# Opening attention of two batches: three copies per head pair and the joining of two heads' rows as SBUF-to-SBUF transfers

## The chip, the core and the metric

The kernel runs on one core of one Trainium2 chip. The metric is the device time of the launch in microseconds. Three runs of the kernel before gave 1260.57, 1261.91 and 1268.36 us; the median is 1261.91 us.

## The reference

Attention with normalized q and k feeds two feed-forward layers. The inputs are 4 batches of 12 heads, 448 positions and 64 columns a head. The change touches the attention of the first two batches alone.

```python
def _attn_ref(q, k, v, g_q, g_k):
    def rmsnorm(x, g):
        rms = np.sqrt(np.mean(x * x, axis=-1, keepdims=True) + 1e-06)
        return x / rms * g
    q_n, k_n = (rmsnorm(q, g_q), rmsnorm(k, g_k))
    scale = 1.0 / np.sqrt(q.shape[-1])
    scores = scale * np.matmul(q_n, k_n.transpose(0, 1, 3, 2))
    scores = scores - np.max(scores, axis=-1, keepdims=True)
    attn = np.exp(scores)
    attn = attn / (np.sum(attn, axis=-1, keepdims=True) + 1e-09)
    return np.matmul(attn, v).astype(np.float32)

def reference(...):
    attn_out = _attn_ref(...)                       # (4, 12, 448, 64)
    x = attn_out.transpose(0, 2, 1, 3).reshape(1792, 768)
    g = x @ w_gate;  x = (g * sigmoid(g) * (x @ w_val)) @ w_out
    h = x @ w_in;    return (h * np.cos(h)) @ w_out2
```

## The kernel before, in words

The attention is done for pairs of heads, called groups here: 6 groups a batch, 24 in all. Groups 0 to 11 (the first two batches) are done in an opening stage of their own, in which the feed-forward layers begin only near the end; the later twelve are woven into the feed-forward layers. The change is in the opening stage.

The order of the program in that stage is by a step number `n`. Every group has 7 score tiles (`NS` = 7) and so takes 7 steps; `c_step(n)` (L785) emits what belongs to a step, and each operation of group g stands at a fixed offset from step 7g. The offsets of the preparation are the third dictionary of `OFF` (L85), less 12 (`CSH`); the offsets behind the products are `CEND` (L804), counted from step 7g + 8 (`CXX`). SP's queue of DMAs and POOL run exactly in that order, each waiting at its head; PE, DVE and ACT run in an order that a scheduler makes out of it when the kernel is built.

For one group the stage does this:

- `p_load` (L317) loads q and k in float32 into `rqk`; `p_sq`, `p_pow`, `p_mul` normalize; `p_khi`, `p_klo`, `p_qhi`, `p_qlo` split into a float16 high and low part in `h16`.
- `c_T` (L656) has the DMA transpose `h16` into `T`: 7 tiles of q and 7 of k, each with its high part on rows 0 to 63 and its low part on rows 64 to 127.
- `c_copy` (L661), the operation `sw` of the table, makes three copies of 64 rows by 896 float16: on DVE the low part of q into rows 0 to 63 of a tile `B` (L666), and the high part of q over the low part in `T` (L667); on ACT the high part of k into rows 0 to 63 of a tile `C` (L668).
- `c_s` (L670) makes the 7 score tiles with `T` on both sides (matmul `s<-T`), and DVE takes the maximum of each row (L680). `c_row` (L682) turns the maxima into a row by small products (`s<-id,cw`, after DVE's two operations L687 and L688) that ACT writes into rows 64 to 127 of `B` (L693).
- `c_st` (L697) makes the transposed scores minus the maximum, with `T` and then with `C` and `B` (matmuls `c<-T` and `c<-cB,cC`), and ACT takes the exponential (L713). `c_av` (L715) multiplies by v, with columns of ones beside it: one PSUM bank has head 0's output on rows 0 to 63 and its sums below, the other has the sums above and head 1's output on rows 64 to 127.
- `c_x` (L725) copies both banks to two tiles `ov` (named `co` in the rows). `c_sum` (L743) sends the sums by DMA into a 64 by 7 form, `c_inv` inverts (L752, L753), `c_out` (L755) writes the inverses to DRAM (`rc<-sm`), `c_back` (L760) reads them back onto all rows (`cr<-rc`), and `c_mul` (L766) with `c_half` (L770) multiplies each half of 64 rows by them (L774) and splits the product for the feed-forward layers (L775, `c_lo`).

Beside this the stage loads weights (`raw`), converts some of them on DVE (L936 to L938, L969) and stores them (`scr_gate`, `scr_val`). `v` goes to tiles `cV` in five DMAs a group.

The two functions on which the steps rest most are these:

```python
        nc.vector.tensor_copy(Bq[:HP], T[HP:, :NS])
        nc.vector.tensor_copy(T[HP:, :NS], T[:HP, :NS])
        nc.scalar.activation(C[:HP], T[:HP, NS:], AF.Copy)
...
        for rows, src in ((slice(0, P), ov),) if g == NC - 1 else ((slice(0, HP), ov[0]), (slice(HP, P), ov[1])):
            nc.vector.tensor_tensor(xs[rows], src[rows], r[rows], op=ALU.mult)
...
    CEND = ((c_x, 0), (c_sum, 1), (c_inv, 3), (c_out, 4), (c_back, 6), (c_mul, 8), (c_lo, CXL))
```

Of the kernel before, what the change touches and what calls it, by code (L numbers as in the profile page):

```python
# [14 lines left out]
AF = mybir.ActivationFunctionType  # L15
ALU = mybir.AluOpType
AX = mybir.AxisListType
PSUM = bass.MemoryType.PSUM
A0 = {'raw0': 2, 'h160': 1, 'sq0': 1, 'pr0': 6, 'T0': 2}
COL = {'B': 3, 'C': 3, 'w': 3, 'r': 1, 'o': 4, 'V': 2}  # L20
A1 = {'p16': 2, 'PT': 1, 'sq': 1, 'pr': 3, 'sm': 10, 'R': 1, 'rv': 1, 'raw': 1, 'h16': 1, 'T': 2}
CF = ('kl xl ql qm kf', 'rp vh nm xl qm sa 2', 'ql xl 0 2 5 6', 'ql xl 0 3 4 6')
LA = 5
# [14 lines left out]
CXL = 11  # L38
# [2 lines left out]
CC2 = 29  # L41
NPH = 3
EARLY = 75
PREL = 33
HPRE = (5, 3)
LO = 3
# [6 lines left out]
for _n, _w in ((67, ("load", 8)), (70, ("load", 9)), (74, ("conv", 8)), (78, ("conv", 9))):  # L53
# [13 lines left out]
  'T': -2,  # L67
  'vhi': -4,
  'vlo': -3,
  'sw': -1},  # L70
 {'load': -23,
  'vload': -21,
  'sqk': -18,
# [7 lines left out]
  'T': -7,  # L81
  'vhi': -10,
  'vlo': -4,
  'sw': -5},
 {'load': -23,  # L85
  'vload': 6,
  'sqk': -18,
  'sqq': -18,
  'pow': -15,
  'mul': -15,  # L90
  'khi': -15,
  'klo': -11,
  'qhi': -14,
  'qlo': -9,
  'T': -6,
  'vhi': -10,
  'vlo': -4,
  'sw': -2},
 {'load': -13,
  'vload': -12,  # L100
  'sqk': -11,
# [7 lines left out]
  'T': -4,  # L109
  'vhi': -6,  # L110
  'vlo': -2,
  'sw': -2},
 {'load': -11,
  'vload': -10,
  'sqk': -9,
# [7 lines left out]
  'T': -4,  # L123
  'vhi': -4,
  'vlo': -3,
  'sw': -2},
 {'load': -16,
  'vload': -14,
  'sqk': -14,
# [7 lines left out]
  'T': -6,  # L137
  'vhi': -7,
  'vlo': -5,
  'sw': -4})  # L140
DEL = ({'phi': 4, 'plo': 4, 'pt': 5, 'sum': 8, 'r': 8, 'av0': 8, 'av1': 9, 'av2': 9, 'av3': 10, 'x': 11},
# [30 lines left out]
def kernel(ctx: ExitStack, tc, q, k, v, g_q, g_k, w_gate, w_val, w_out, w2_in, w2_out, out):  # L172
    nc = tc.nc
    in_order = set()
    sync = InOrder(tc, nc.sync, "SP", in_order)
# [3 lines left out]
    B, H, S, D = q.shape  # L179
    P = 128  # L180
    CO = 384
    NP = H // 2
    NC = 2 * NP
# [8 lines left out]
    HP = P // 2  # L192
# [30 lines left out]
    def xy_tile(more=False):  # L223
        return xy_pools[int(more)].tile([P, 2, S], F16, tag="xy", name="xy")

    def tmp():
        return tmp_p.tile([P, S], F32, tag="tmp", name="tmp")
# [70 lines left out]
    NS = 2 * S // P  # L298
# [3 lines left out]
    prep = {}  # L302
# [320 lines left out]
    colc = {}  # L623
    CT = [(0, 0), (1, 0), (0, 1), (1, 1), (0, 2), (1, 2), (None, 3)]

    def ctile(nm, shape, dt, g=None):
        return c_p.tile(shape, dt, tag="c" + nm, name="c" + nm, bufs=COL[nm])

# [32 lines left out]
    def c_copy(g):  # L661
        pg = prep[g]
        T = pg["T"]
        Bq = pg["B"] = ctile("B", [P, NS, P], F16)
        C = colc[g % 3][0]
        nc.vector.tensor_copy(Bq[:HP], T[HP:, :NS])  # L666
        nc.vector.tensor_copy(T[HP:, :NS], T[:HP, :NS])  # L667
        nc.scalar.activation(C[:HP], T[:HP, NS:], AF.Copy)  # L668

    def c_s(n):  # L670
        g, t = divmod(n, NS)
# [43 lines left out]
    def c_av(g, j):  # L715
        pg = prep[g]
        if j == 0:
            pg["o"] = (bank(ps_t, "t"), bank(ps_u, "u"))
        for h in range(2):
            hs = slice(HP * h, HP * h + HP)  # L720
            rows = slice(0, P) if j < 3 else hs
            e = col[g, 2 * j + h] if j < 3 else col[g, NS - 1]
            pe.matmul(pg["o"][h][:, :S], colv[g % 2][rows, j, h], e[rows], start=(j == 0), stop=(j == 3))
# [31 lines left out]
    def c_out(g):  # L755
        pg = prep[g]
        rd = pg["rd"] = dram.tile([2, S], F32, name=f"rc{g}")
        sync.dma_start(rd.rearrange("h (p s) -> (h p) s", s=NS), pg["r"][:, 2, :NS])

    def c_back(g):  # L760
        pg = prep[g]
        R = pg["R"] = ctile("r", [P, S], F32)
        for h in range(2):
            sync.dma_start(R[HP * h:HP * h + HP], pg["rd"][h].partition_broadcast(HP))
# [5 lines left out]
    def c_half(g, ov, r):  # L770
        x = X[g] = xy_tile()
        xs = tmp()
        for rows, src in ((slice(0, P), ov),) if g == NC - 1 else ((slice(0, HP), ov[0]), (slice(HP, P), ov[1])):
            nc.vector.tensor_tensor(xs[rows], src[rows], r[rows], op=ALU.mult)  # L774
        nc.scalar.activation(x[:, 0], xs, AF.Copy)  # L775
        if g == NC - 1:
            gps.tensor_sub(x[:, 1], xs, x[:, 0])
        xlo[g] = xs
# [6 lines left out]
    def c_step(n):  # L785
# [3 lines left out]
        if m >= 0 and m % NS in (1, 3, 5, 6) and m < NCB:  # L789
            c_av(m // NS, (1, 3, 5, 6).index(m % NS))  # L790
        for f, d in CEND:
            m = n - CXX - d
# [8 lines left out]
        if n < NCB:  # L801
            s_prep(n)

    CEND = ((c_x, 0), (c_sum, 1), (c_inv, 3), (c_out, 4), (c_back, 6), (c_mul, 8), (c_lo, CXL))  # L804

    PREP = (
        ("load", p_load), ("vload", p_vload), ("sqk", lambda g: p_sq(g, 1)), ("sqq", lambda g: p_sq(g, 0)),
        ("pow", p_pow), ("mul", p_mul), ("khi", p_khi), ("klo", p_klo),
        ("qhi", p_qhi), ("qlo", p_qlo), ("T", p_T), ("sw", p_sw), ("vhi", p_vhi), ("vlo", p_vlo),
    )  # L810
    TAIL = (("sum", a_sum), ("r", a_r), ("av0", lambda g: a_av(g, 0)), ("av1", lambda g: a_av(g, 1)), ("av2", lambda g: a_av(g, 2)),
            ("av3", lambda g: a_av(g, 3)), ("x", a_x))
# [1 line left out]
    def ph(g):  # L814
        return 2 if g < NC else 2 + g // NP
# [3 lines left out]
    def s_prep(n):  # L819
        for nm, f in PREP:  # L820
            for g in range(NPAIR):
                if NS * g + OFF[ph(g)][nm] - (CSH if g < NC else 0) == n:
                    if g < NC and nm in ("vhi", "vlo"):
                        continue
                    if g < NC and nm == "vload":
                        c_v(g)
                    elif g < NC and nm == "T":
                        c_T(g)
                    elif g < NC and nm == "sw":
                        c_copy(g)  # L830
                    else:
                        f(g)
# [585 lines left out]
    for n in range(1 - LEAD, NCB + CXX + CXL + 1):  # L1418
# [6 lines left out]
        if n in (CC1 - LEAD, CC2 - LEAD):  # L1425
            c_const(1 if n == CC1 - LEAD else 2)
        if n == EARLY:
            in_order.add("PE")
        i = n - EARLY
        if 0 <= i < KX:  # L1430
# [40 lines left out]
    for bn, per in blocks:  # L1471
# [15 lines left out]
        for qn in range(per):  # L1487
# [8 lines left out]
            if bn == B and qn % 2 == 0:  # L1496
                pre_step(qn < PREL)
            for it in sched.get(qn, ()):
# [145 lines left out]
```

## Time and profile before

| what | value |
|---|---|
| runs | 1260.57, 1261.91, 1268.36 us; median 1261.91 us |
| the profiled execution | 1267.07 us, of which 1265.3 us from the first to the last instruction |
| PE busy | 1171.3 us (93%), 6292 matmuls; mean granted clock 0.984 of full |
| DVE busy | 962.1 us (76%), 1824 instructions |
| ACT busy | 688.5 us (54%), 1317 instructions |
| POOL busy | 380.9 us (30%), 309 instructions |

Busy times are of one execution. A matmul's end is modelled, so that PE's busy time counts some waiting as work; the share of busy time says less than who waited for whom. Register, semaphore and DMA-issuing instructions are not counted as busy, but SP's issues have rows of their own with the time that each held the queue. The opening stage lies between about 21 us (the first matmul) and 228 us (the first `mm` matmul) of the span.

### The profile page before, as it was taken

How to read it: one execution, taken by the hardware profiler on the slowest of the kernel's cores; microseconds unless marked ns; L12 is line 12 of the kernel's file. 1: busy time of each engine (PE TensorE's matmuls, PEld its weight loads, DVE VectorE, ACT ScalarE, POOL GpSimd, SP SyncE). 2: the span in 40 equal slices, each digit the busy share in tenths (PEclk: the TensorE clock that was granted, in tenths of full speed). 3: DMA queues.
4: the chain of work that ended last, by engine and by line, in shares of the span. 5: the costliest groups of instructions: out<-in, count | busy, mean ns of one | idle time of the engine just before them, and what ended most of it. 6: DMA issues, size and time to landing. Idle time of an engine off the chain costs nothing. (4 is left out here: it accounts for less than half of the span.)

```text
span 1265.3 us, 18148 instructions
## 1 busy us (share of the span) xinstructions
PE 1171.3 (93%) x6292; PEld 658.6 (52%) x6292; DVE 962.1 (76%) x1824; ACT 688.5 (54%) x1317; POOL 380.9 (30%) x309
## 2 busy tenths in 40 slices
PE   1798788998989998999999999999999999999998
PEld 0333333453765445944458654775555554666655
DVE  5987876789778998258863499747888788999882
ACT  3676655554466552455664247447667767666220
POOL 7644412435421354224554111521221121100000
PEclk9999889998999999999999999999999999999999
DMA  5645666567777878689857688771522245132122
GB/s 150 185 127 133 166 163 209 96 168 209 212 215 217 208 235 244 213 190 210 190 129 222 235 291 304 239 244 66 195 80 68 74 159 195 57 106 76 51 69 88
DMA packets 220780, 211.53 MB, mean 167 GB/s; under 512 B 147600, under 2 KB 178192, under 8 KB 220688
## 3 DMA queue, kind: packets, MB, share of 16 engines
q1 hardware_dynamic: 220688, 210.38, 57.5%
q8 instruction: 49, 0.80, 0.3%
q14 instruction: 43, 0.35, 0.1%
HBM read 138.44 MB, written 41.57 MB: 142 GB/s over the span
## 5 line engine op out<-in xcount | busy, mean ns | idle before, releaser
L163 PE MATMUL mm<-xy,wp 128*128 128x448 f16 x2484 | 493.5, 355 | 5.4 <-ACT co L735 2.5
L163 PEld LDWEIGHTS <-wp 128*128 128x128 f16 x2880 | 278.3, 99 | 279.6 <-issue 36.0
L163 PE MATMUL mm<-g,wp 128*128 128x448 f32 x864 | 183.6, 370 | 1.7 <-DVE ga L1142 1.7
L163 PEld LDWEIGHTS mm<-g,wp 128*128 128x128 f32 x864 | 161.1, 189 | 19.8 <-issue 4.7
L163 PEld LDWEIGHTS <-g 128*128 128x128 f16 x840 | 82.1, 98 | 55.3 <-DVE tmp L163 0.8
L163 POOL TENSOR_TENSOR g<-ga,g 128x448 fp32r<-128x448 f32 x48 | 64.8, 1364 | 146.1 <-ACT g L1144 145.8
L163 POOL TENSOR_TENSOR g<-tmp,g 128x224 f16<-128x224 f32 x64 | 47.8, 750 | 197.9 <-ACT g L1261 197.6
L508 ACT ACTIVATE pr<-s,sm,esc 128x448 f32<-128x448 f32 x84 | 60.3, 719 | 78.0 <-DVE sm L502 70.6
L163 PE MATMUL s<-T 128*64 128x448 f16 x336 | 63.9, 397 | 40.7 <-DVE T L667 22.9
L163 POOL TENSOR_TENSOR wp<-w,wp 128x768 fp32r<-128x768 f32 x36 | 70.2, 1954 | 58.3 <-ACT wp L1025 38.9
L163 PEld LDWEIGHTS <-T 128*64 128x64 f16 (+1 forms) x432 | 28.6, 109 | 111.1 <-issue 82.7
L936 DVE TENSOR_SCALAR w<-raw 128x768 int32<-128x768 int32 x68 | 47.0, 694 | 49.8 <-POOL wp L163 16.7
L498 DVE TENSOR_REDUCE sm<-s 128x1 f32<-128x448 f32 x84 | 51.1, 614 | 35.4 <-PE s L163 35.3
L163 POOL TENSOR_TENSOR ri<-ss,half 128x14 f32<-128x14 f32 x24 | 64.4, 2685 | 39.4 <-DVE ss L357 29.7
L938 DVE SCALAR_TENSOR_TENSOR w<-raw,w 128x768 int32<-128x768 int32 x68 | 73.9, 1088 | 0.6
L937 DVE SCALAR_TENSOR_TENSOR w<-raw,w 128x768 int32<-128x768 int32 x68 | 73.3, 1081 | 0.6
L956 ACT ACTIVATE raw<-w 128x768 f32<-128x768 f32 x56 | 47.0, 839 | 45.0 <-DVE w L938 31.6
L163 POOL TENSOR_TENSOR p<-pr,p 128x448 f16<-128x448 f32 x36 | 42.0, 1172 | 88.7 <-ACT p L532 69.8
L1254 ACT ACTIVATE tmp<-tmp 128x448 f32<-128x448 f32 x64 | 36.4, 571 | 49.8 <-DVE tmp L1253 48.5
L163 PE MATMUL mm<-wp,g 128*128 128x384 f16 x360 | 62.1, 326 | 0.5 <-DVE tmp L163 0.4
L713 ACT ACTIVATE pr<-c,esc 128x448 f32<-128x448 f32 x84 | 50.4, 629 | 21.3 <-PE c L163 21.2
L163 PE MATMUL s<-wp,g 128*128 128x384 f16 x360 | 61.9, 326 | 0.0
(201 smaller groups left out, 2017.8 us busy)
## 6 DMA issues: line engine op xcount, KB each, us to landing
raw<-in_moe_w_out_dram SPq DMA_DIRECT2D x28, 768.0 KB, 5.2
raw<-in_moe_w_in_dram SPq DMA_DIRECT2D x16, 768.0 KB, 5.6
raw<-in_moe_w_gate_dram SPq DMA_DIRECT2D x12, 768.0 KB, 6.1
raw<-in_moe_w_val_dram SPq DMA_DIRECT2D x12, 768.0 KB, 5.9
wp<-scr_gate SPq DMA_DIRECT2D x24, 384.0 KB, 4.4
w<-scr_out SPq DMA_DIRECT2D x24, 384.0 KB, 4.0
wp<-scr_val SPq DMA_DIRECT2D x24, 384.0 KB, 5.3
y<-tmp SPq DMA_DIRECT2D x30, 224.0 KB, 3.9
```

Of the source, the lines that this page charges most:

```text
L163: r = f(*args, **kw)
L498: nc.vector.tensor_reduce(sm[:, 0, t:t + 1], slot[n][:, :S], axis=AX.X, op=ALU.max)
L508: nc.scalar.activation(e, slot.pop(n)[:, :S], AF.Exp, bias=sm[:, 1, t:t + 1], scale=esc, accum_out=sm[:, 2, t:t + 1],)
L713: nc.scalar.activation(e, ps[:, :S], AF.Exp, scale=esc)
L936: nc.vector.tensor_scalar(wi, hi, 3, 0x3FFFFFF8, op0=ALU.logical_shift_left, op1=ALU.bitwise_and)
L937: nc.vector.scalar_tensor_tensor(wi, hi, -0x40000000, wi, op0=ALU.bitwise_and, op1=ALU.bitwise_or)
L938: nc.vector.scalar_tensor_tensor(wi, lo, 29, wi, op0=ALU.logical_shift_right, op1=ALU.bitwise_or)
L956: nc.scalar.activation(sq_dst[0], w32, AF.Square, accum_out=n[:, 0:1])
L1254: nc.scalar.activation(r, r, AF.Abs)
```

## The change

For every group but the first (`NFIRST` = 1), the three copies of `c_copy` become DMAs inside SBUF, in two operations: `sw` sends the low part of q to `B`, and a new operation `dup`, three steps later, sends the high part of q over the low part in `T` and the high part of k to `C`. Group 0 keeps its three engine copies. The preparation of a group in this stage starts one step earlier, the transpose two steps earlier, `sw` three, and there are four buffers of `B` in place of three. A new `c_join` sends head 1's 64 rows from the second `ov` into the first, over the sums there, so that one product of 128 rows takes the place of two of 64; it stands at offset 5 of `CEND`, between the write of the inverses and their reading back. Group 11, the last of the stage, keeps its own way through `c_x`.

```diff
-COL = {'B': 3, 'C': 3, 'w': 3, 'r': 1, 'o': 4, 'V': 2}
+COL = {'B': 4, 'C': 3, 'w': 3, 'r': 1, 'o': 4, 'V': 2}
...
+NFIRST = 1
...
- {'load': -23,
+ {'load': -24,
...
-  'T': -6,
+  'T': -8,
...
-  'sw': -2},
+  'sw': -5,
+  'dup': -2},
...
         C = colc[g % 3][0]
-        nc.vector.tensor_copy(Bq[:HP], T[HP:, :NS])
-        nc.vector.tensor_copy(T[HP:, :NS], T[:HP, :NS])
-        nc.scalar.activation(C[:HP], T[:HP, NS:], AF.Copy)
+        if g < NFIRST:
+            nc.vector.tensor_copy(Bq[:HP], T[HP:, :NS])
+            nc.vector.tensor_copy(T[HP:, :NS], T[:HP, :NS])
+            nc.scalar.activation(C[:HP], T[:HP, NS:], AF.Copy)
+        else:
+            sync.dma_start(Bq[:HP], T[HP:, :NS])
+
+    def c_dup(g):
+        if g >= NFIRST:
+            T = prep[g]["T"]
+            sync.dma_start(T[HP:, :NS], T[:HP, :NS])
+            sync.dma_start(colc[g % 3][0][:HP], T[:HP, NS:])
...
+    def c_join(g):
+        ov = prep[g]["ov"]
+        sync.dma_start(ov[0][HP:], ov[1][HP:])
...
-        for rows, src in ((slice(0, P), ov),) if g == NC - 1 else ((slice(0, HP), ov[0]), (slice(HP, P), ov[1])):
-            nc.vector.tensor_tensor(xs[rows], src[rows], r[rows], op=ALU.mult)
+        nc.vector.tensor_tensor(xs, ov if g == NC - 1 else ov[0], r, op=ALU.mult)
...
-    CEND = ((c_x, 0), (c_sum, 1), (c_inv, 3), (c_out, 4), (c_back, 6), (c_mul, 8), (c_lo, CXL))
+    CEND = ((c_x, 0), (c_sum, 1), (c_inv, 3), (c_out, 4), (c_join, 5), (c_back, 6), (c_mul, 8), (c_lo, CXL))
```

The other entries of that dictionary from `sqk` to `qlo` go one step earlier as well.

SP's queue in the order of the program, one group of the kernel before, from one transpose to the next (`h` is `h16`, `sm` the sums and their inverses, `rc` the inverses in DRAM, `cr` these on all rows, `rqk` and `cV` the loads of q, k and v; a trailing x2 is two such DMAs):

```order
L163 DMA_TRANSPOSE T<-h_825 128x14x128
L163 DMA rc_1060<-sm 128x7
L163 DMA cr<-rc_1060 64x448 x2
L163 DMA rqk<-in_k_dram 64x448 x2
L163 DMA rqk<-in_q_dram 128x448
```

The same stretch of SP's queue in the changed kernel:

```order
L170 DMA_TRANSPOSE T<-h_806 128x14x128
L170 DMA sm<-co 64x1x7 x2
L170 DMA cB<-T 64x896
L170 DMA rc_1070<-sm 128x7
L170 DMA co<-co 64x448
L170 DMA rqk<-in_k_dram 64x448 x2
L170 DMA rqk<-in_q_dram 128x448
L170 DMA cr<-rc_1070 64x448 x2
L170 DMA T<-T 64x896
L170 DMA cC<-T 64x896
```

Four DMAs are new in each group. The reading back of the inverses, which stood directly behind their writing, now stands behind the join and the three loads of q and k, and the transpose stands ahead of the two sends of the sums.

DVE's queue around the maxima and the row of one group before, from the inverse of an earlier group's sums to the second operation of the row (`cw`):

```order
L753 RECIPROCAL sm<-sm 128x7
L680 TENSOR_REDUCE sm<-s 128x1 x2
L408 TENSOR_TENSOR rqk<-rqk,ri 128x448
L938 SCALAR_TENSOR_TENSOR w_1111<-raw,w_1111 128x768
L680 TENSOR_REDUCE sm<-s 128x1
L666 COPY cB<-T 64x896
L774 TENSOR_TENSOR tmp<-co,cr 64x448
L687 TENSOR_SCALAR cw<-sm 128x7
L667 COPY T<-T 64x896
L774 TENSOR_TENSOR tmp<-co,cr 64x448
L688 SCALAR_TENSOR_TENSOR cw<-sm,cw 128x7
```

The same stretch of DVE's queue in the changed kernel, and the product that follows:

```order
L769 RECIPROCAL sm<-sm 128x7
L696 TENSOR_REDUCE sm<-s 128x1 x3
L703 TENSOR_SCALAR cw<-sm 128x7
L704 SCALAR_TENSOR_TENSOR cw<-sm,cw 128x7
L357 TENSOR_REDUCE ss<-sq 128x7
L370 TENSOR_TENSOR rqk<-rqk,gk 128x448
L357 TENSOR_REDUCE ss<-sq 128x7
L793 TENSOR_TENSOR tmp<-co,cr 128x448
```

The copies are gone, the product with the inverses (L793, before L774) is one of 128 rows and stands behind the row, and nothing but maxima stands between the inverse and the row.

## Rows read from the trace of the kernel before

**Rows 1.** Busy by stretch: us, busy of PE, PEld, DVE, ACT, POOL, clock, DMA, GB/s.
```profile
120.00:140.00 20.00, 11.42 (x45) 4.19 (x44) 12.39 (x24) 8.88 (x17) 7.58 (x5) 0.74 0.70 193
40.00:203.00 163.00, 138.68 (x587) 56.34 (x586) 132.04 (x271) 106.90 (x194) 65.03 (x46) 0.93 0.61 164
...
240.00:280.00 40.00, 39.55 (x225) 19.40 (x225) 31.61 (x63) 21.84 (x45) 15.93 (x11) 1.00 0.56 122
```
**Rows 2.** Timeline of PE, row products: start, length, operation, [idle before, releaser].
```profile
39.56 0.95 PE L163 MATMUL s<-id,cw 128*64 128x128 f16 x7
...
202.75 0.58 PE L163 MATMUL s<-id,cw 128*64 128x128 f16 x7 [1.07 <-DVE cw L688]
```
**Rows 3.** Waits of PE, 40 to 228 us: total, times, longest.
```profile
PE s L163 <- DVE sm L680: 14.5, 10, 8.3
...
PE s L163 <- ACT cB L693: 3.2, 7, 0.7
...
PE s L163 <- DVE cw L688: 2.2, 2, 1.1
```
**Rows 4.** Timelines of SP and DVE ahead of the longest wait.
```profile
119.51 1.57 SPq L163 DMA_DIRECT2D raw<-in_moe_w_gate_dram  x1
...
126.95 0.56 DVE L936 TENSOR_SCALAR w<-raw 128x768 int32<-128x768 int32 x1 [6.46 <-DMA raw<-in_moe_w_gate_dram]
```
**Rows 5.** Groups by line, 40 to 228 us: busy, mean ns, idle before.
```profile
L774 DVE TENSOR_TENSOR tmp<-co,cr 64x448 f32<-64x448 f32 x20 | 12.4, 618 | 4.8 <-DMA cr<-rc 4.4
...
L668 ACT ACTIVATE cC<-T 64x896 f16<-64x896 f16 x10 | 9.4, 944 | 6.2 <-DMA T<-h 6.1
...
L666 DVE COPY cB<-T 64x896 f16<-64x896 f16 x10 | 5.2, 519 | 0.6 <-DMA T<-h 0.3
...
L667 DVE COPY T<-T 64x896 f16<-64x896 f16 x10 | 3.9, 386 | 0.3
```
**Rows 6.** Waits of ACT, 20 to 230 us.
```profile
ACT cC L668 <- DMA T<-h: 19.2, 7, 6.8
```
**Rows 7.** Timeline of SP's queue over one group, 60 to 78 us.
```profile
60.03 1.56 SPq L163 DMA_TRANSPOSE T<-h  x1
67.12 0.35 SPq L163 DMA_DIRECT2D rc<-sm  x1
68.59 1.11 SPq L163 DMA_DIRECT2D cr<-rc  x2
69.75 1.23 SPq L163 DMA_DIRECT2D rqk<-in_k_dram  x2
71.02 0.58 SPq L163 DMA_DIRECT2D rqk<-in_q_dram  x1
71.70 3.67 SPq L163 DMA_DIRECT2D cV<-in_v_dram  x5
75.48 1.45 SPq L163 DMA_DIRECT2D sm<-co  x2
77.03 1.56 SPq L163 DMA_TRANSPOSE T<-h  x1
```
**Rows 8.** DMAs, 20 to 230 us: KB each, median us from issue to landing.
```profile
cr<-rc SPq DMA_DIRECT2D x22, 112.0 KB, 2.9
...
sm<-co SPq DMA_DIRECT2D x22, 1.8 KB, 2.0
T<-h SPq DMA_TRANSPOSE x12, 4.4
```
**Rows 9.** Waits of SP's queue, 40 to 228 us: total, times, longest.
```profile
SPq L163 <- DMA rc<-sm: 27.5, 11, 5.1
SPq L163 <- DVE sm L753: 20.5, 7, 5.8
SPq L163 <- POOL h L163: 7.2, 5, 3.0
```

More of the change, by code (lines that the diff above doesn't have):

```diff
@@ L69 @@
   'vlo': -3,
-  'sw': -1},
+  'sw': -1,
+  'dup': -1},
  {'load': -23,
@@ L83 @@
   'vlo': -4,
-  'sw': -5},
- {'load': -23,
+  'sw': -5,
+  'dup': -5},
+ {'load': -24,
   'vload': 6,
[L87 to L94, printed above, removed]
-  'T': -6,
+  'sqk': -19,
+  'sqq': -19,
+  'pow': -16,
+  'mul': -16,
+  'khi': -16,
+  'klo': -12,
+  'qhi': -15,
+  'qlo': -10,
+  'T': -8,
   'vhi': -10,
   'vlo': -4,
-  'sw': -2},
+  'sw': -5,
+  'dup': -2},
  {'load': -13,
@@ L111 @@
   'vlo': -2,
-  'sw': -2},
+  'sw': -2,
+  'dup': -2},
  {'load': -11,
@@ L125 @@
   'vlo': -3,
-  'sw': -2},
+  'sw': -2,
+  'dup': -2},
  {'load': -16,
@@ L139 @@
   'vlo': -5,
-  'sw': -4})
+  'sw': -4,
+  'dup': -4})
 DEL = ({'phi': 4, 'plo': 4, 'pt': 5, 'sum': 8, 'r': 8, 'av0': 8, 'av1': 9, 'av2': 9, 'av3': 10, 'x': 11},
@@ L808 @@
         ("pow", p_pow), ("mul", p_mul), ("khi", p_khi), ("klo", p_klo),
-        ("qhi", p_qhi), ("qlo", p_qlo), ("T", p_T), ("sw", p_sw), ("vhi", p_vhi), ("vlo", p_vlo),
+        ("qhi", p_qhi), ("qlo", p_qlo), ("T", p_T), ("sw", p_sw), ("dup", c_dup), ("vhi", p_vhi), ("vlo", p_vlo),
     )
@@ L822, in s_prep @@
                 if NS * g + OFF[ph(g)][nm] - (CSH if g < NC else 0) == n:
-                    if g < NC and nm in ("vhi", "vlo"):
+                    if nm in ("vhi", "vlo") and g < NC or nm == "dup" and g >= NC:
                         continue
```

## Prediction

> **What bounds the kernel now.** I read the busy times by stretch first. The first matmuls of the feed-forward layers come at about 228 us, and from there PE has hardly a gap: 39.55 us busy of 40 between 240 and 280 us, at full clock [rows 1]. Ahead of that PE is busy 138.68 of 163 us, at a mean clock of 0.93, while DVE has 132.04 us of work in the same 163 us, the most of any engine but PE [rows 1]. So the question is how much shorter the opening stage gets; what follows starts when its last outputs are there, and I let a gain or a loss in the stage pass to the end in full.
>
> Next the pace. The row product of group 0 starts at 39.56 us and that of group 11 at 202.75 us [rows 2]: 163.2 us for 11 periods, 14.84 us each. Then who makes PE wait: between 40 and 228 us it stands 14.5 us for DVE's row maxima and 2.2 us for DVE's two operations of the row, and 3.2 us for ACT [rows 3]. Of the 14.5 us one wait alone is 8.3 us [rows 3], and that one is not DVE's load: a weight tile sent for at 119.51 us came only at 126.95 us, and DVE stood 6.46 us in front of it with the maxima queued behind [rows 4]. What DVE's load explains is thus 14.5 + 2.2 - 8.3 = 8.4 us.
>
> Last SP's queue, which carries every transfer and runs in order. From one transpose at 60.03 us to the next at 77.03 us its issues take 1.56 + 0.35 + 1.11 + 1.23 + 0.58 + 3.67 + 1.45 = 9.95 us of 17.0 us; the rest it waits, most of it ahead of the send of the inverses [rows 7]. SP is the queue to which the change moves work.
>
> **The change part by part.** The sum is against the profiled execution, 1267.07 us, which is 5.16 us above the median 1261.91 of the runs; the forecast is brought to the median by taking those 5.16 us off.
>
> *Engine work that goes.* Eleven groups lose a copy of 0.519 us and one of 0.386 us on DVE [rows 5]: 11 x 0.905 = 10.0 us. Eleven pairs of 64-row products at 0.618 us become one each; I price the 128-row one the same, since it has the same 448 columns, so 11 x 0.618 = 6.8 us more goes [rows 5]. DVE loses 16.8 us; the 20 copies and half of the 20 products in the row of 40 to 228 us are 5.2 + 3.9 + 6.2 = 15.3 us, 12% of the 132.04 us of the stretch. ACT loses 11 x 0.944 = 10.4 us [rows 5], and with these copies the 19.2 us in which ACT, in order, stood in front of a transpose that had not landed, its exponentials behind it [rows 6].
>
> *What that is worth on PE.* The bounds are nothing, if something else is late next, and the whole 16.8 us, if DVE's throughput is the pace. Between them stand the 8.4 us that PE waits for DVE's load. In the changed order of DVE the row stands right behind the maxima, with no copy and no product ahead of it, so I take three quarters of the 8.4 us: -6.3 us. For ACT I take half of the 3.2 us: -1.6 us. Part of the stage runs at the lower clock level (a mean of 0.93 over 163 us, 0.74 between 120 and 140 us, where the 8.3 us wait lies [rows 1]); with fewer stalls some of it returns. The loss at the lower level is 7% of 163 us, 11.4 us; the stalls that go are a third of those above, and the longest stays, so I take a sixth: -1.9 us.
>
> *Issues that SP gains.* Four a group, 44 in all. The nearest row is the reading back of the inverses, also 64 rows and 112 KB: 1.11 us for two, 0.555 each [rows 7]; a load of 128 rows takes 0.58. So +44 x 0.555 = 24.4 us of issuing, 2.2 us a group.
>
> *A wait that SP loses.* The reading back stood right behind the writing of the inverses and held SP 27.5 us in 11 waits, 2.5 us each [rows 9]. Now the join and three loads stand between, 0.555 + 1.23 + 0.58 = 2.4 us of issues, which cover it while there are loads of q and k for this stage (by the offsets to step 41, 44 steps behind the first row product, so in 7 of the 11 periods), and 0.6 us of it after: 7 x 2.4 + 4 x 0.6 = 19 us go.
>
> *A wait that SP gains.* The send to `B` must wait until the transpose has landed, 4.4 us from its issue [rows 8], with only the transpose's own 1.56 us and the sums' 1.45 us between: 1.4 us a group where SP is late, 15 us in all, and nothing where SP arrives by its steps, since three steps of 14.84 / 7 = 2.1 us lie between. Queued behind it are the inverses, the join, the loads of q and k, the reading back and the other two copies. In the same place SP waits 20.5 us today for DVE's inverse [rows 9], and a wait for both is only as long as the longer. Bounds 0 and +15 us on SP; I take 6.
>
> *The second hop.* The copy over `T` must wait for the send to `B` (it overwrites what that reads), which is hidden under the inverses and the loads, and then has two steps, 4.2 us, before the scores want it. A transfer of this size lands in 2.0 to 2.9 us by the nearest rows [rows 8]. If SP is late by more than 4.2 - 0.6 - 2.9 = 0.7 us, the scores' matmul stands at PE's head, with the products of the other group behind it. Bounds: 0 and 11 x 2.9 = 32 us; I take +1.5 us on PE, since before the copies too depended on the same queue, and SP's total changes by 24.4 - 19 + 6 = +11 us of 163, of which it waits about 40% today [rows 7].
>
> *The transfers themselves.* 44 x 112 KB are 5 MB more on the 16 DMA engines, which are busy 0.61 of the stretch and move 164 GB/s [rows 1]: over 163 us some 31 GB/s more, and I price it at nothing, with room as the cover; where the engines are full, as around the weight tiles, a landing gets longer, which the 1.5 us hold.
>
> *Start.* Group 0 keeps its copies, so the first matmul stays. The opening has one step more ahead of it, which has only loads in it: 0.
>
> Sum: -6.3 - 1.6 - 1.9 + 1.5 = -8.3 us, 1267.07 - 8.3 = 1258.8 us for such an execution, less 5.16 is 1253.6; I say **1254 us**.
>
> In the rows an issue is no small thing: two reads of 112 KB hold SP 1.11 us and land after 2.9 us [rows 7, 8], and issues fill 9.95 us of a 17.0 us period. The Trainium skill, "DMA: Bandwidth & Descriptors", section "Issuing engines are not separate DMA queues", says that the sequencer's time to start a DMA is usually small beside the DMA itself. By that rule the 24.4 us would count as nothing, SP would wait as now and the rival in which SP is the bound would fall away; the trace does not agree for transfers of this size, and I keep the rival.
>
> **The rivals.**
>
> *DVE's throughput is the pace, and all of its relief comes back.* For it: DVE has 132 of 163 us of work and PE's longest total is for it [rows 1, 3]. Against it: SP's floor. For a group SP would need 9.95 + 4 x 0.555 + 1.4 = 13.6 us [rows 7, 8] and the share of the weights. These are by the code 24 loads and stores in the stage; an issue of 128 rows takes 0.35 us (the inverses) to 0.58 us (q) [rows 7], and with 0.45 us, near the middle, they make 1.0 us a group. That is 14.6 us with loads of q and k, 12.8 us without their 1.8 us; seven periods of the one and four of the other are 153 us, 10 us below 163.2. So the stage can hardly give back more than 10 us in its pace, and with 4 us of clock and of the tail it is 14: 1262 - 14 = 1248 us.
>
> *The relief is hidden anyway.* The long waits hang on transfers: the 8.3 us [rows 3, 4], and 4.4 us of DVE's products with the inverses [rows 5]. Against it: only one of PE's ten waits for the maxima is that long. If DVE merely waits longer in front of the transfers, 1262 us.
>
> *SP becomes the bound (slower).* The mechanism: SP's period rises above 14.84 us, and the scores, the loads and the weights all come late. Its floor of 14.6 us holds if SP waits for nothing but its own transposes, so it decides from about 0.25 us of other waiting per group. SP waits today 7.2 us for POOL's low parts and 20.5 us for DVE's inverses [rows 9]; if all of the first and half of the second stay, 17 us, the eleven periods take 153 + 17 = 170 us, and with two groups whose scores find their copy late by a landing of 2.9 us [rows 8], 176 to 177 us: 14 us more than now, 1276 us. Against it: a queue that is late finds its waits already over.
>
> **How the numbers follow.** My forecast has a chance of 0.50, the full relief 0.19, the hidden one 0.18, the slower one 0.13. About 1% (12.6 us) is what a measurement of this kernel tells from no change: below 1249.3 faster, above 1274.5 slower. Of my forecast's cases a seventh (0.07) lie below 1249.3, of the full relief nearly all (0.17); of the slower rival three quarters (0.10) lie above 1274.5, and of the others 0.02. So faster 0.24, same 0.64, slower 0.12. The range runs from 1243 us (the 16.8 us of DVE and 2 us of clock) to 1273 us (where the slower rival begins): 0.05 is left out below and 0.13 above.
>
> **What would show it.** Right: the row products of groups 0 and 11 lie about 156 us apart in place of 163.2, PE's wait for the row maxima falls from 14.5 towards 9 us, ACT waits for no transpose, and SP's wait for the inverses' writing falls to about 9 us. Wrong on the slow side: PE's or its weight load's waits name the copy over `T`, DVE waits longer for weight tiles or for q and k, SP's wait for the transpose is above 2 us a group. Wrong on the fast side: the eleven periods fall to 150 us or less. If the stage shrinks and the total does not, the gain was lost behind 228 us, in the transfers of the weights.

## The result and the profile after

The changed kernel takes 1282.02 us (median of 4 runs, 1279.95 to 1282.85); beside it the kernel before took 1263.09 us (4 runs, 1260.57 to 1268.36). The ratio is 1.0141, with a 95% interval of 1.0116 to 1.0166: **slower by 1.4%**, some 18 us. The forecast was 1254 us, in a range from 1243 to 1273.

The page of the changed kernel's profile, span and busy times:

```profile
span 1280.9 us, 18205 instructions
...
PE 1173.2 (92%) x6292; PEld 658.3 (51%) x6292; DVE 946.9 (74%) x1791; ACT 680.0 (53%) x1306; POOL 380.2 (30%) x309
```

DVE is relieved by 962.1 - 946.9 = 15.2 us and ACT by 8.5 us. The engine work went about as priced, and the span is 15.6 us longer all the same.

Where the loss arises is in the timeline of PE in the changed kernel: the row products of groups 0 and 11 and the first `mm` matmul of the feed-forward layers.

```profile
41.08 1.03 PE L170 MATMUL s<-id,cw 128*64 128x128 f16 x7
...
216.25 0.58 PE L170 MATMUL s<-id,cw 128*64 128x128 f16 x7
...
242.75 3.57 PE L170 MATMUL mm<-xy,wp 128*128 128x448 f16 x18 [2.47 <-ACT co L751]
```

And the same `mm` matmul in the kernel before:

```profile
227.70 4.68 PE L163 MATMUL mm<-xy,wp 128*128 128x448 f16 x15 [2.49 <-ACT co L735]
```

The eleven periods take 216.25 - 41.08 = 175.2 us where they took 163.2 [rows 2]: 15.9 us a group for 14.84. Group 0 is 1.5 us later, the `mm` matmul 15.05 us, the end 15.6 us. So next to nothing was lost behind the opening stage. Its busy times by stretch in the changed kernel:

```profile
40.00:203.00 163.00, 132.53 (x546) 52.86 (x546) 108.35 (x229) 92.02 (x170) 60.40 (x44) 0.90 0.66 174
...
255.00:295.00 40.00, 38.57 (x219) 19.17 (x221) 32.89 (x65) 22.53 (x48) 16.30 (x11) 1.00 0.53 126
```

In the 163 us that [rows 1] show, DVE has 108.35 us of work in place of 132.04, ACT 92.02, PE 132.53 in place of 138.68, at a granted clock of 0.90 in place of 0.93. Every engine gets less done in the same time, so no engine's load alone sets the pace. From the row product of group 0 to that of group 11, PE is busy 142.73 us with 587 matmuls, at a clock of 0.89, where before it was 138.87 us with 586, at 0.93: by these modelled times about 4 of the 12.0 us are slower matmuls, and the other 8 are waiting. Who PE waits for in the stage, 40 to 243 us (total, times, longest):

```profile
PE s L170 <- DVE sm L696: 12.1, 5, 8.3
PE s L170 <- DMA T<-T: 7.1, 4, 2.4
PE s L170 <- DVE vrow L393: 5.8, 2, 3.1
PE s L170 <- ACT cB L709: 4.8, 7, 1.0
```

The wait for the maxima, 14.5 us in [rows 3], is hardly shorter, and 8.3 us of it are still one wait. New are the copy over `T`, 7.1 us, and the row of v's maxima (`vrow`, part of the scaling of v and no part of the change), 5.8 us in the row above and 1.6 us more at L389; neither is among PE's waits before. ACT is rid of its waits for transposes, 19.2 us in [rows 6]; the one that is left is group 0's own copy:

```profile
ACT cC L676 <- DMA T<-h: 6.3, 1, 6.3
```

DVE's product with the inverses, one of 128 rows, takes what one of 64 rows took (618 ns in [rows 5]), and DVE waits longer in front of it than in [rows 5], 9.3 us for 4.4:

```profile
L793 DVE TENSOR_TENSOR tmp<-co,cr 128x448 f32<-128x448 f32 x10 | 6.2, 622 | 9.3 <-DMA cr<-rc 9.3
```

Now SP's queue over one group of the changed kernel, from one transpose to the next:

```profile
118.82 1.55 SPq L170 DMA_TRANSPOSE T<-h  x1
120.46 1.70 SPq L170 DMA_DIRECT2D sm<-co  x2
122.87 0.49 SPq L170 DMA_DIRECT2D cB<-T  x1
125.99 0.34 SPq L170 DMA_DIRECT2D rc<-sm  x1
126.43 0.39 SPq L170 DMA_DIRECT2D scr_val<-wp  x1
126.91 0.49 SPq L170 DMA_DIRECT2D co<-co  x1
127.45 1.24 SPq L170 DMA_DIRECT2D rqk<-in_k_dram  x2
128.73 1.49 SPq L170 DMA_DIRECT2D rqk<-in_q_dram  x1
130.27 0.43 SPq L170 DMA_DIRECT2D raw<-in_moe_w_gate_dram  x1
130.80 1.12 SPq L170 DMA_DIRECT2D cr<-rc  x2
131.96 0.60 SPq L170 DMA_DIRECT2D T<-T  x1
132.65 0.54 SPq L170 DMA_DIRECT2D cC<-T  x1
133.29 3.38 SPq L170 DMA_DIRECT2D cV<-in_v_dram  x5
136.78 1.57 SPq L170 DMA_TRANSPOSE T<-h  x1
```

Its issues take 13.8 us of 17.96, where they took 9.95 of 17.0 in [rows 7]; 0.8 us of the 13.8 are for weights, which that other stretch did not have. From `co<-co` on no gap is longer than 0.14 us; what is left of waiting lies around the send to `B` and the inverses. What SP waits for in the stage, 40 to 243 us:

```profile
SPq L170 <- DMA rc<-sm: 16.4, 6, 3.5
SPq L170 <- DVE sm L769: 13.1, 7, 3.4
SPq L170 <- DVE vrow L393: 5.5, 2, 3.8
SPq L170 <- DMA T<-h: 4.9, 6, 2.3
```

The wait for the writing of the inverses fell from 27.5 to 16.4 us and that for DVE's inverses from 20.5 to 13.1 [rows 9]; the one for the transpose is new. Adding up the time of every single issue on SP between the row products of groups 0 and 11 gives the queue's whole account; the waits between two issues of one kind, which a merged row (x2, x5) takes in, count as idle. It is made for the experiments too, each from one profiled execution, and the comparisons below use it:

| kernel | SP issues, us | SP idle, us | the eleven periods, us | ratio of the whole time |
|---|---|---|---|---|
| before | 103.6 | 59.6 | 163.2 | 1 |
| after | 121.4 | 53.8 | 175.2 | 1.0141 |
| before + 44 issues of 16 bytes a row | 123.7 | 51.5 | 175.2 | 1.0141 |
| the same, engines' order held | 127.8 | 52.3 | 180.1 | 1.0152 |
| before, in that kernel's order, without its issues | 100.6 | 60.1 | 160.8 | 1.0035 |
| before, q and k one step earlier | 109.7 | 63.7 | 173.4 | 1.0062 |
| before + the join alone | 104.1 | 49.5 | 153.6 | 0.9941 |
| after, v loads on ACT's queue | 93.9 | 72.3 | 166.2 | 1.0012 |
| the same, in the changed kernel's order | 96.2 | 81.1 | 177.3 | 1.0119 |

From before to after SP issues 17.8 us more and idles 5.8 us less, and the stage is 12.0 us longer. The two columns add up to the periods in every row by construction, so this account names no cause; the experiments have to. The profiled execution of the order without its issues (1262.81 us) was the fastest of its twelve, 8.6 us below their median, so its 160.8 us are on the low side.

### The profile page after: what moved, and what is told of

It reads as the page before. It is cut to its first block, busy times and chain, and to the rows that moved or that the text cites. A ratio compares the mean times of both kernels' runs of the same rounds, so it can differ in the third digit from the quotient of the medians.

```text
span 1280.9 us, 18205 instructions
## 1 busy us (share of the span) xinstructions
PE 1173.2 (92%) x6292; PEld 658.3 (51%) x6292; DVE 946.9 (74%) x1791; ACT 680.0 (53%) x1306; POOL 380.2 (30%) x309
## 5 line engine op out<-in xcount | busy, mean ns | idle before, releaser
L955 DVE TENSOR_SCALAR w<-raw 128x768 int32<-128x768 int32 x68 | 46.5, 686 | 54.7 <-POOL wp L170 20.3
L170 POOL TENSOR_TENSOR xy<-tmp,xy 128x448 f16<-128x448 f32 x24 | 27.6, 1151 | 119.8 <-ACT xy L794 90.7
```

The lines of the kernel that those rows point to most:

```text
L170: r = f(*args, **kw)
L955: nc.vector.tensor_scalar(wi, hi, 3, 0x3FFFFFF8, op0=ALU.logical_shift_left, op1=ALU.bitwise_and)
```

## The experiments

Theory 1: the 44 issues on SP's queue are the price, whatever they carry. Rivals: the new sends wait for each other and the scores for them; the moved offsets; the transfers' load; and, later, the other order that the scheduler makes for PE, DVE and ACT. Each run has its own runs of the kernel before on the same chip; ratios are to those.

**The join taken out of the changed kernel** (`e1_no_join`).

```diff
-    def c_join(g): ...
-        nc.vector.tensor_tensor(xs, ov if g == NC - 1 else ov[0], r, op=ALU.mult)
+        for rows, src in ...:
+            nc.vector.tensor_tensor(xs[rows], src[rows], r[rows], op=ALU.mult)
```

> The changed kernel without the join of the two heads' rows: the product with the inverses is two of 64 rows again, 11 transfers fewer, DVE 6.8 us more. Theory 1 (SP's queue is the pace: every issue of 0.5 us in it lengthens the stage): a quarter of the 44 issues goes, with the wait they cause, so 4 to 6 us faster than the changed kernel, 1276 to 1278 us; DVE's 6.8 us more cost nothing. Theory 2 (the scores wait for the second hop, the copy over T): the join stands ahead of that copy in the queue, so 0 to 2 us faster, 1280 to 1282 us. Theory 3 (DVE's load is the pace): slower than 1282 us.

1.0143 (1.0105 to 1.0182), as with the join. Eleven issues fewer and eleven products more on DVE came out even. Theory 1's 4 to 6 us did not come, but they lie within the interval; no theory is favoured.

**44 transfers that nobody reads, added to the kernel before**: three where the copies stand and one where the join stands, for groups 1 to 11; once of 112 KB (`e2_dummies`), once of 16 bytes a row (`e7_tiny`).

```diff
         C = colc[g % 3][0]
+        if g:
+            for k in range(3):
+                c_fake(g, k)
...
+    def c_fake(g, k):
+        sync.dma_start(dram.tile([HP, 8], F16, name=f"fd{g}_{k}"), fake[0][:HP, :8])
```

> The kernel before, with all its engine copies, and 44 more transfers of 112 KB that nothing reads, at the places of the kernel before's copies (three) and of the join (one), for groups 1 to 11; they go from SBUF to DRAM and wait for nothing. Theory 1: SP's issues alone cost the time, so 12 to 20 us slower than before, 1275 to 1283 us, with no wait of the scores for a copy. Theory 2: nothing waits for these transfers, so within 4 us of before. A rival of both, that the scheduler's new order or the moved offsets are the cause: also near 1263 us.

> The run of 44 added transfers that nothing reads, again on the kernel before, now with 16 bytes a row in place of 1792: as many issues in SP's queue at the same places, and next to no bytes. If the issues are the price (theory 1): still 10 to 18 us slower than before, a ratio of 1.008 to 1.014. If it was the load on the DMA engines, or the ring that lets a transfer go only when the eighth before it has landed: within 4 us of before.

1.0131 (1.0104 to 1.0158) and 1.0141 (1.0105 to 1.0178). All engine copies are still there, nothing reads the added transfers, and the loss is that of the change. Bytes play no part that these runs show: 1 KB costs what 112 KB costs. The other rival of the second run, the ring, is not settled by small transfers, since they take as long to land (a median of 3.5 us against 2.9). The traces settle it: in the changed kernel no gap over 0.15 us in SP's queue ends when the eighth transfer before has landed (within 0.25 us), in the kernel before two do, of 3.0 us together, so that the ring is not the change's price.

**One such issue a group** (`e11_dose`).

> The kernel before with one added transfer of 16 bytes a row in each of eleven groups, at the place of the engine copies, in place of four a group. Theory 1 in proportion: a quarter of the 17 us of the run with 44, so 3 to 6 us slower than before, ratio 1.002 to 1.005. With a threshold: within 2 us of before.

1.0039 (1.0022 to 1.0056): 0.0039 x 1264 us = 4.9 us for 11 issues, 0.45 us each; the 44 of the run before cost 0.0141 x 1269 = 17.9 us, 0.41 us each. The price goes with the count.

**The five v loads of a group on another queue**: from the changed kernel on ACT's (`e3_after_cv_act`) and on POOL's (`e3p_after_cv_pool`), from the kernel before likewise (`e4_before_cv_act`, `e4p_before_cv_pool`).

```diff
-            sync.dma_start(V[:HP, :4 - h, h, hs], src[:, 0:NS - h:2])
+            nc.scalar.dma_start(V[:HP, :4 - h, h, hs], src[:, 0:NS - h:2])
...
```

> The changed kernel with the five loads of v a group issued from ACT's queue in place of SP's: SP loses 3.3 us of issues a group, more than the 2.1 us that the change put on it; ACT gets them. Theory 1: the stage gets its pace back, 1258 to 1266 us, if ACT's issues do not become the next bound. Theory 2: the copy over T still comes two hops behind the transpose, 1277 to 1283 us.

> The kernel before with the five loads of v a group issued from ACT's queue. Theory 1, taken on to the kernel before: SP's issues are 108 of 163 us there, so 38 us of issues less make it 5 to 12 us faster than before, unless ACT's issues cost as much. If SP is no bound in the kernel before: within 4 us of it.

On ACT's queue: after 1.0012 (0.9994 to 1.0031), before 0.9997 (0.9978 to 1.0015). The change's loss is gone, but the kernel before gains nothing, where theory 1 gave 5 to 12 us: issues moved from SP's queue to ACT's bring it nothing, while issues added to SP's cost. What the moved issues cost on ACT's queue is not parted from that.

> The changed kernel with the loads of v issued from POOL's queue. Theory 1: as with ACT's queue, the loss of 1.4% goes, and without ACT's issues the engine work that the change saved may show: 0 to 10 us faster than before. Theory 2 (the scores wait for the second hop): 1277 to 1283 us, a ratio above 1.010.

> The same with the loads of v issued from POOL's queue, which has 65 us of work in 163: POOL waits in order, so its low parts and the transposes behind them may come later. Theory 1: 5 to 12 us faster than before; if POOL's order stalls: slower by 5 us or more.

On POOL's: after 1.0092 (1.0065 to 1.0120), before 1.0085 (1.0053 to 1.0116). Theory 1 misses both (0 to 10 us and 5 to 12 us faster than before): the loads on POOL cost the kernel before 0.0085 and give the changed one back about 0.005 of its 0.0141. Why they cost on POOL was not followed up.

**The moved offsets**: once with engine copies in the changed kernel's table (`e5_table`, `NFIRST = 12`), once the changed kernel with the old table (`e9_old_offsets`).

```diff
- {'load': -24,
+ {'load': -23,
...
-  'T': -8,
+  'T': -6,
...
-  'sw': -5,
+  'sw': -4,
```

> The changed kernel with all twelve groups on the engine copies: the moved offsets, four buffers of B and the join stay, 33 transfers go. Theory 1: 11 issues a stage remain of 44, so 4 to 6 us above before, 1266 to 1269 us. Theory 2: no second hop, so 1262 to 1265 us. A rival, that the moved offsets (the transpose ahead of the sends of the sums) are the cause: 1277 us or more.

1.0178 (1.0156 to 1.0199), outside what theory 1 said and where the rival of the moved offsets put it. The run tells little, since in that table the engine copies stand only three steps behind the transpose. ACT's wait for the transposes, 20 to 255 us, is above the 19.2 us of [rows 6], and PE waits 9.9 us for ACT's copy:

```profile
ACT cC L676 <- DMA T<-h: 34.9, 9, 8.7
```

> The changed kernel with the offsets of the kernel before for the preparation (load, transpose and the rest), the send to B two steps behind the transpose and the other two copies where the engine copies were. The transposes stand behind the sends of the sums again, and the loads behind the reading back of the inverses. Theory 1: the same 44 issues, so a ratio of 1.010 to 1.017. Theory 3 (the moved offsets are the cause): 1.005 or less.

1.0144 (1.0117 to 1.0171), the same as after: with the old offsets the loss is there all the same, so they are not the cause.

**Loads of q and k between the writing and the reading of the inverses, in the kernel before** (`e10_load24`, `'load': -24`), the place that the prediction credited with 19 us.

> The kernel before with only the loads of q and k one step earlier, so that in SP's queue they stand between the write of the inverses and their reading back, as in the changed kernel; nothing else differs. Theory 1 with the prediction's step on the wait that SP loses: SP's wait for the inverses' write falls from 27.5 to 12 us or less, and the stage gets 4 to 10 us shorter, 0.992 to 0.997 of before. If the wait only moves to another place of the queue: within 2 us of before.

1.0062 (1.0043 to 1.0081), slower, where theory 1 gave 0.992 to 0.997. SP's waits in it, 40 to 228 us:

```profile
SPq L163 <- DVE wp L969: 16.9, 4, 9.1
SPq L163 <- DMA rc<-sm: 16.1, 6, 3.6
SPq L163 <- POOL h L163: 13.9, 4, 6.8
```

The wait for the inverses' writing falls from 27.5 to 16.1 us, as it does in the changed kernel, and waits for a weight's split and for POOL's low part take its place: SP's idle time is 63.7 us, not less than the 59.6 us before. The wait was covered, and others took its place in the same queue. The scheduler's order was free here, and no run parts its share.

**The join alone** (`e6_join_only`): the kernel before with `c_join` and the product of 128 rows, its copies and table as they were.

```diff
+    def c_join(g):
+        ov = prep[g]["ov"]
+        sync.dma_start(ov[0][HP:], ov[1][HP:])
...
-        for rows, src in ...:
-            nc.vector.tensor_tensor(xs[rows], src[rows], r[rows], op=ALU.mult)
+        nc.vector.tensor_tensor(xs, ov if g == NC - 1 else ov[0], r, op=ALU.mult)
```

> The kernel before with the join and the 128-row product alone: 11 issues more, DVE 6.8 us less, the engine copies and all offsets as before. Theory 1 (issues in SP's queue are the price, in proportion): 3 to 5 us slower than before, ratio 1.002 to 1.004. If the price comes only above a threshold of SP's load: within 2 us of before. If DVE's load were the pace: 3 to 6 us faster.

1257.52 us against 1264.29, a ratio of 0.9941 (0.9918 to 0.9963): **faster than both kernels**. Theory 1 missed; the nearest forecast is that of DVE's load as the pace (3 to 6 us faster). DVE's relief alone is not enough for it, though: the join on ACT's queue, below, has the same relief and is slower than before. Its row products and its longest wait of PE:

```profile
39.94 0.95 PE L163 MATMUL s<-id,cw 128*64 128x128 f16 x7
...
193.58 0.58 PE L163 MATMUL s<-id,cw 128*64 128x128 f16 x7
```
```profile
PE s L163 <- DVE sm L680: 6.8, 7, 2.1
```

The periods take 153.6 us, and the wait for the maxima is halved from 14.5 us; the wait of 8.3 us is gone. Eleven issues more, but each stands behind the writing of the inverses, where SP waited anyway: its issues take 104.1 us against 103.6 in a shorter stretch, and its idle time falls by 10.1 us.

**33 bare issues of 16 bytes a row beside the join** (`e12_join_33`).

> The join and the one 128-row product of the change, engine copies and preparation as before, and at the place of the three copies three unused transfers of 16 bytes a row for each of groups 1 to 11: the 44 issues of the changed kernel without the copies' own waits. Theory 1 (each issue on SP's queue costs about 0.4 us, and the copies' waits cost nothing beyond): 33 x 0.4 = 13 us more than the join alone (0.9941), a ratio of about 1.0045, while the changed kernel is at 1.0141. If it falls at 1.0045 the other 0.010 (12 us) of the changed kernel belong to the copies' own waits for the transpose and for each other. Rival (the issues are all): the same as the changed kernel, about 1.014. Rival (the join only moved a gain that issues do not touch): 0.994 to 0.997.

1.0104 (1.0071 to 1.0137): 0.0163 above the join alone, 20.6 us for 33 issues, 0.62 us each and half as much again as expected. The changed kernel, whose 33 sends do the copies' work, is at 1.0141 (1.0116 to 1.0166); the two intervals overlap. So the sends cost about what bare issues cost: their own waits (7.1 us of PE, 4.9 us of SP) and the relief of DVE and ACT together make no difference that these runs tell from nothing. The two may also cancel; no run parts them.

**One copy by transfer beside the join** (`e13_join_cC`), and **the join on ACT's queue** (`e15_join_act`).

```diff
-        nc.scalar.activation(C[:HP], T[:HP, NS:], AF.Copy)
+        if g:
+            sync.dma_start(C[:HP], T[:HP, NS:])
+        else:
+            nc.scalar.activation(C[:HP], T[:HP, NS:], AF.Copy)
```

```diff
-        sync.dma_start(ov[0][HP:], ov[1][HP:])
+        nc.scalar.dma_start(ov[0][HP:], ov[1][HP:])
```

> The join and the 128-row product, and of the three copies only the one of the high part of k to C as a transfer: ACT loses 11 x 0.94 us and its wait for the transpose, SP has 22 added issues in place of 11. Theory 1: 0.9941 + 0.0039 (eleven issues) = 0.998. Rival (ACT's relief comes back on PE, up to the 3 us that it waits for ACT): 0.995 or below, and then this is the best version. Rival (the copy's wait for the transpose at SP's head costs as much as the issue): 1.002.

> The join and the 128-row product, the join issued from ACT's queue in place of SP's. Theory 1: SP is relieved of eleven issues, about 4 us less than the join alone, 0.990 to 0.991, if ACT's own issues cost nothing. Rival (ACT, held by its own order of work, pays for the issues): 0.994 to 0.998. The kernel with the join on SP's queue was at 0.9941.

1.0063 (1.0047 to 1.0079) and 1.0050 (1.0032 to 1.0069): both slower than the join alone, and both miss what theory 1 gave (0.998 and 0.991). Eleven transfers to `C` cost 0.0122, three times a bare issue, and a queue with eleven issues fewer was no help. For the join on ACT's queue the trace shows a price: ACT, which takes its instructions in order, stands 11.3 us in three waits for the sums' sends, whose rows the join overwrites, the longest with exponentials behind it:

```profile
ACT pr L713 <- DMA sm<-co: 5.6, 1, 5.6
```

The kernel before and the join on SP's queue have no such wait. SP's count of issues, then, is not all, and one suspect is left: each edit so far had also let the scheduler order PE, DVE and ACT anew.

**The order held.** Three kernels in which the instructions of the engines are tied, one to the next, in the order of another kernel: the kernel before with 44 issues of 16 bytes a row in its own old order (`e16_issues_same_order`); the kernel before without them, in the order that the kernel with them had (`e17_order_only`); the changed kernel with the v loads on ACT's queue and the changed kernel's order on PE, DVE and POOL (`e18_after_order_cv_act`).

```diff
     with _tile.TileContext(nc, schedule_with_timeline_sim=True) as tc:
         tile_attention_moe_kernel(tc, *args)
+        pin_order(tc, SKIP)
```

> The kernel before with the order of its instructions on PE, DVE, ACT and POOL held as it is, one by one, and the 44 added transfers of 16 bytes a row at the copies' and the join's places of SP's queue. In the earlier runs with added transfers the scheduler that orders PE, DVE and ACT had made another order as well. Theory 1 (SP's time for the issues is the price): 1.010 to 1.015, as with the order left free (1.0141). Rival (the order that the scheduler makes of it is the price): 1.000 to 1.003.

1.0152 (1.0124 to 1.0180), 0.0152 x 1267 us = 19.3 us or 0.44 us for each of 44 issues. Its row products:

```profile
39.42 0.95 PE L164 MATMUL s<-id,cw 128*64 128x128 f16 x7
...
219.55 0.96 PE L164 MATMUL s<-id,cw 128*64 128x128 f16 x7 [5.54 <-DVE cw L692]
```

and a piece of its SP queue, in which `fd` are the added issues:

```profile
119.26 1.33 SPq L164 DMA_TRANSPOSE T<-h  x1
125.02 0.34 SPq L164 DMA_DIRECT2D rc<-sm  x1
125.46 0.37 SPq L164 DMA_DIRECT2D scr_val<-wp  x1
125.89 0.49 SPq L164 DMA_DIRECT2D fd<-id  x1
126.43 0.58 SPq L164 DMA_DIRECT2D raw<-in_moe_w_gate_dram  x1
127.55 2.21 SPq L164 DMA_DIRECT2D cr<-rc  x2
129.80 1.24 SPq L164 DMA_DIRECT2D rqk<-in_k_dram  x2
131.08 0.59 SPq L164 DMA_DIRECT2D rqk<-in_q_dram  x1
131.71 1.79 SPq L164 DMA_DIRECT2D fd<-id  x3
```

> The kernel before with no transfer added, its instructions on PE, DVE, ACT and POOL held in the order that the kernel with 44 added transfers of 16 bytes a row had. Theory 1 (the issues are the price): 0.998 to 1.003. Rival (the order is the price): 1.010 to 1.015. If both this and the kernel with the issues in the old order are in between, the loss divides between them.

1.0035 (1.0015 to 1.0055). So for the kernel before the issues are the price, and the order that goes with them costs little by itself; the run also bounds what the tying costs, since it is tied as well. Beside the kernel before, the one with 44 issues and the old order held (1.0152) has 24.2 us more of issues on SP in the periods; its idle time gave way by 7.3 us, and the periods grew by 16.9.

The piece of the queue suggests why the waits hardly take the issues up. What SP waits for between 120 and 126 us of it:

```profile
SPq L164 <- DVE sm L757: 4.4, 1, 4.4
```

The 4.4 us between the transpose, whose issue ends at 120.59 us, and `rc<-sm` at 125.02 are for a chain that SP itself began with the sums' send, and that goes through DVE, where the inverse stands in order behind maxima, a weight's split and the copy to `B`; DVE has no gap there. Three added issues at 131.71 us delay the next sums' send by their whole 1.79 us, and the chain behind it with them. An issue between the two ends of such a wait is covered, like the one at 125.89 us, between the writing and the reading of the inverses. That is a reading of the rows; no run moved the three issues into a gap.

> The changed kernel with the loads of v on ACT's queue, as in the run that came out at 1.0012, but with the order of the changed kernel held on PE, DVE and POOL (ACT's order is made anew, since it has the loads to issue). Theory 1: SP's relief alone brings the loss back, 1.000 to 1.003. Rival (that run was fast for its other order): 1.010 to 1.014.

1.0119 (1.0087 to 1.0151), against 1.0012 with the order free. SP issues 96.2 us and idles 81.1 us here, less issuing than in the kernel before, and the loss is there all the same. So it was not SP's relief alone that brought the changed kernel back; an order made for it belongs to it, worth 0.0107. Nor is SP free in it: it waits 16.8 us for DVE's inverses, 13.4 for transposes, and for the v loads that ACT issues, which nothing in SP's queue reads:

```profile
SPq L171 <- DMA cV<-in_v_dram: 8.6, 4, 5.5
```

Whether the loss is there because the held order was made for a late SP, or because ACT with the v loads in its queue doesn't fit it, stays open, and with it how much of the changed kernel's own loss is its order; so does how much of the join's 0.0059 is its own order, and what the dear 0.0122 of the copies to `C` is made of.

## Why the prediction was wrong

**The step that failed** is the pricing of SP's total: "SP's total changes by 24.4 - 19 + 6 = +11 us of 163, of which it waits about 40% today", for which I put 1.5 us on PE, because the other 40% would absorb it. They did not: the eleven periods are 12.0 us longer, and with the 1.5 us ahead of group 0 and 1.5 us behind group 11 the first `mm` matmul comes 15.05 us later. That SP's idle share is no such room is shown by 44 bare issues, for which nothing waits, with the engines' old order held: the idle time took up 7.3 us of their 24.2, and the time rose to 1.0152. Why it is no room, that much of the rest are latencies which the same queue starts and then waits for in order, is a reading of the rows. The +11 itself came close by luck: the issues were 17.8 us in place of 24.4, the wait for the inverses' writing fell by 11 us in place of 19, and the wait for the transposes was 4.9 in place of 6, which makes +12. How much of the changed kernel's loss is the order that the scheduler made for it stays open.

**Terms of the sum, one by one.**

- *Engine work that goes.* Near: DVE -15.2 us in the whole (predicted 16.8), ACT -8.5 (10.4), and the 128-row product costs 622 ns (priced 618).
- *What it is worth on PE, -6.3 and -1.6 us.* Wrong: the wait for the maxima fell by 2.4 us, the one for ACT's row of `B` rose by 1.6, and 7.4 us of waits for v's row came. In the changed kernel the join's relief of DVE and its eleven issues came out even (1.0143 without it, 1.0141 with it); alone, the join gave 0.9941.
- *Clock, -1.9 us.* Wrong in sign: the stretch of 40 to 203 us ran at 0.90, not above 0.93, beside more waiting of PE; in the eleven periods that is about 4 us more for the same matmuls.
- *Issues, +24.4 us.* Near: 0.49 to 0.60 us each in the rows above, as priced. The 39 of them between the two row products take 20.8 us; the net is +17.8, mostly because the transposes' issues take 15.6 us there in place of 20.0.
- *The wait that goes, -19 us.* Too large: 27.5 to 16.4 us is -11, and the run with the loads moved alone shows that even such a fall need not shorten the queue's account.
- *The wait that comes, +6 us, bounds 0 and 15.* Near: 4.9 us.
- *Second hop, +1.5 us of 0 to 32.* Too small: PE waits 7.1 us for the copy over `T`. The run with 33 bare issues loses nearly as much (1.0104) with no such wait, so the loss does not need it.
- *The transfers themselves, nothing.* Right within the intervals: 16 bytes a row cost as much as 112 KB.

**The rivals.** "SP becomes the bound" at 1276 us came nearest, with 0.13 too low a chance; its periods of 176 to 177 us were 175.2. The argument against it, that a queue that is late finds its waits already over, is the failed step once more: SP's idle time fell by 10%, not to nothing. Its floor of 153 us counted only SP's wait for the transposes; the issues alone are 121.4 us in the changed kernel, 11.0 a group, and 4.9 us a group of waiting remain. SP's wait for DVE's low part of k (`h`, 12.0 us before, 40 to 228 us) is in none of its terms; 2.2 us of it are left in the changed kernel, 40 to 243 us. The rule of the Trainium skill ("DMA: Bandwidth & Descriptors", section "Issuing engines are not separate DMA queues"), by which the time to start a DMA is usually small beside the DMA itself, was weighed and set aside there; yet the sum left SP next to no effect on PE. The trace: an issue of 594 ns stands beside a landing of 3.5 us for 1 KB, about a sixth, and small beside the DMA is not small for the kernel, for these issues cost 0.41 to 0.44 us each of the whole time.

**What was to be seen.** The row products are 175 us apart, not 156; PE's wait for the maxima is 12.1 us, not 9, and SP's wait for the inverses' writing 16.4, not 9; only ACT's waits for transposes went as forecast. Of the signs named for the slow side two came: PE's waits name the copy over `T`, and DVE's wait for weight tiles (L936 before, L955 after) rose from 11.5 us to 18.1. The third did not: SP's wait for the transpose is 0.4 us a group, below the 2 us that I named.

## What to carry to other kernels

Do not take a queue's idle share as room. Count its issues and the latencies that it starts and then waits for in order as one serial time per period; by the reading of the rows here, issues are covered where they fit between the two ends of such a wait. Before moving engine work into transfers, add the bare issues, with tiny transfers and the engines' order held; and try each part of a change alone, since here one transfer of four gained 0.6% and all four together lost 1.4%. Where a scheduler orders the engines, every edit also changes that order, so hold it when an effect of about 1% is to be put down to a cause.

## What the runs showed of the hardware that was not expected

An issue's time on SP's queue did not depend on the bytes: the added issues of 64 rows, of 112 KB in the first run and of 1 KB in the second, held it equally long (ns, shortest, median, longest).

```profile
L163 SPq DMA_DIRECT2D fd<-fk x44: 446/590/1332, 29.8 to 242.6; - x44
```
```profile
L163 SPq DMA_DIRECT2D fd<-fk x44: 445/594/1333, 29.7 to 244.9; - x44
```

SP's and ACT's transfers use the same eight semaphores in turn, and in none of the runs' traces does an issue start before the transfer that last used its semaphore has landed; so a load moved to ACT's queue can hold up SP, as the 8.6 us above show. And these transfers inside SBUF take about as long to land as the reads of DRAM, 2.2 to 3.7 us; the landings in the changed kernel, 20 to 245 us (KB each, median us from issue to landing):

```profile
cr<-rc SPq DMA_DIRECT2D x22, 112.0 KB, 3.0
...
cB<-T SPq DMA_DIRECT2D x11, 112.0 KB, 2.2
T<-T SPq DMA_DIRECT2D x11, 112.0 KB, 2.9
cC<-T SPq DMA_DIRECT2D x11, 112.0 KB, 2.6
co<-co SPq DMA_DIRECT2D x11, 112.0 KB, 3.7
```
